# A recurrence and two layers on one core: a new order of the slots in the chunk periods

## The chip, the cores and the metric

One Trainium2 chip, one core of it. The metric is the device time of one execution in microseconds; the kernel is one program with one launch.

## What is computed

A recurrence over 768 positions for 4 x 8 heads of 40 channels, then two feed-forward layers on its output. Cut to what matters:

```python
for t in range(S):                     # S = 768, state is 40 x 40 per head
    y[:, :, t] = einsum('bhd,bhde->bhe', rt, state)
    Sa = einsum('bhde,bhe->bhd', state, at)
    state = state * wt[:, :, None, :] - einsum('bhd,bhe->bhde', Sa, bt) \
            + einsum('bhd,bhe->bhde', vt, kt)
x = y.transpose(0, 2, 1, 3).reshape(3072, 320)
h = x @ w_in;   x = square(relu(h)) @ w_out      # layer 0, 2048 hidden
h = x @ w_in2;  out = (h * cos(h)) @ w_out2      # layer 1
```

All inputs are drawn anew per seed; the weights of the layers come as 64-bit floats and are turned into 32-bit ones on the chip.

## The kernel before, in words

The 768 positions are cut into 12 chunks of 64. For each chunk the kernel forms decay products (`decay`, scans on DVE), products of the inputs with one another (`gt`, line 407, PE, tile pgt, then two masked multiplications into ga on DVE), stores parts of ga to DRAM (`gt_out`, Ls), loads them back in another layout (`solve_load`, L) and inverts 32 x 32 triangles (`solve`: 31 pairs of a product ttmp, line 448, and a sum T, line 451, each waiting for the one before, all on DVE). The result goes through DRAM again (`solve_store`, `load_t`) and is merged with two sets of small PE products (`merge`, tiles pw and pt). Then `state` takes four groups of heads through five steps each: pq, px, pu, py, pm on PE, with copies on ACT after pq, px and pm and multiplications on DVE after pu (into mov) and py (into MT, sz, yt). `pmat` (tile pp) makes a further operand. `y_store` writes the chunk's output.

All of it is written out by hand, no scheduler reorders it: `period(c)` is cut into 42 slots, and the calls `at(t, f, ...)` say what is issued in slot t. In period c the state of chunk c, the solve of chunk c+1 and the first steps of chunks c+2 and c+3 are issued. Each engine takes its instructions strictly in this order, so an instruction that waits holds up all that stands behind it on its engine. That goes for the DMA queue of SP too, on which all loads and stores of the periods stand.

Three further streams run beside it, slot by slot:

- The weights. `first`, `rest` and `second` (all through `stages`) load a piece, clamp it (ACT, then DVE), join the bits (DVE), add (POOL, tile u, line 179) and end it: for layer 0 by `split` (ACT into ws, line 206, and POOL), for layer 1 by a store to w2f. The tuples give the slot of each step within a job.
- The solve's links. `rate[t]` is the credit of a slot: after each operation that another part issues on DVE, one link of the solve follows, up to the credit.
- The layers (`Mlp.stream`). From slot FIRST of period 2 on, each slot issues RATE = 64.2/42 units of the stream. A unit of layer 0 is two PE products of 512 columns; a step has 8 units: 8 products into h, the activation (three operations on ACT, gh, and gl on POOL), and 8 products po of the step before the last. A block is 512 tokens (two chunks) and 16 steps; at its end the next block's input is split (xh on ACT, xl on DVE), once `load_x` has brought it and `ready` allows it.

After the last period the rest of the stream runs alone: layer 0 to its end, then layer 1 (lines 839 and 785).

Of the kernel before, what the change touches and what calls it, by code (L numbers as in the profile page):

```python
# [154 lines left out]
class Weights:  # L155
# [57 lines left out]
    def first(self, last=NF):  # L213
# [3 lines left out]
        def job(f):  # L217
# [17 lines left out]
            for t, c0, n in ((5, 0, 384), (6, 384, DM)):  # L235
                out.append((t, lambda c0=c0, n=n: begin(c0, n)))
                if self.raw:
                    out += [(t + 1, lambda c0=c0, n=n: self.bits(st["w"][:, c0:c0 + n], st[c0])),
                            (t + 2, lambda c0=c0, n=n: self.add(st["w"][:, c0:c0 + n], st[c0], st[c0]))]
                out.append((t + 2, lambda c0=c0: self.split(st["dst"], st[c0], c0)))  # L240
            return out
# [3 lines left out]
    def pieces(self, nm, tiles, period, end):  # L245
# [4 lines left out]
        def job(f, c0, n):  # L250
            st = {}

            def load():
                st["w"] = self.p.tile([128, 256, 2], I32, tag="w", name="w", bufs=2)[:, 0:n]
                self.load(nm, f, st["w"], c0)

            def clamp():
                st["u"] = self.p.tile([128, 256], F32, tag="u", name="u", bufs=2)[:, 0:n]
                self.clamp(st["w"], st["u"])

            return [(0, load), (5, clamp), (6, lambda: self.bits(st["w"], st["u"])),
                    (7, lambda: self.add(st["w"], st["u"], st["u"])), (period + 4, lambda: end(f, c0, st["u"]))]

# [18 lines left out]
class Attn:  # L282
# [159 lines left out]
    def solve(self):  # L442
        nc, L, T = self.nc, self.L, self.T
        for j in range(31):
            r, n = j // 2 + 1, 31 - j
            tmp = self.p2.tile([128, 136], F32, tag="ttmp", name="ttmp", bufs=1)
            tv = tmp[:, 0:r * n].rearrange("p (a b) -> p a b", b=n)
            nc.vector.tensor_tensor(tv, T[:, 0:r, j:j + 1].to_broadcast([128, r, n]),  # L448
                                    L[:, j:j + 1, j + 1:32].to_broadcast([128, r, n]), op=ALU.mult)
            yield  # L450
            nc.vector.tensor_tensor(T[:, 0:r, j + 1:32], T[:, 0:r, j + 1:32], tv, op=ALU.add)  # L451
            yield
        self.tn = L[0:64, 0:16].rearrange("p a b -> p (a b)").rearrange("p (i k) -> p i k", k=16)
        nc.vector.tensor_copy(self.tn, T[0:64].rearrange("p k i -> p i k"))
        yield
# [421 lines left out]
ALONE = 2  # L877
FIRST, RATE = 23, 64.2 / 42


class Program:
# [52 lines left out]
    def run(self):  # L934
# [46 lines left out]
        for k in range(10):  # L981
            self.vec.credit = 6
            if k in (3, 4, 5, 6, 7, 9):
                step(g1)
# [3 lines left out]
            if k in (1, 3, 5):  # L988
                step(self.w1)
            self.vec.finish()  # L990
        self.vec.credit = 100
        self.vec.finish()
        A.solve_store()
        A.load_t()
# [14 lines left out]
    def period(self, c):  # L1009
# [9 lines left out]
        for half in range(2):  # L1019
            for k in range(5):  # L1020
                for q in range(2):
                    at(20 * half + 4 * k + 2 * q, step, st[2 * half + q])
        for h, t0 in enumerate((5, 6) if c == 0 else (2, 4) if more else (4, 12)):
            mg = A.merge(h)
            at(t0, step, mg)
            at(t0 + 2, step, mg)
        at(2, A.rv_load, c, 2)
        at(6, A.rv_load, c, 3)
        at(6, A.mov_load, c, 2)
        at(9, A.pmat, c, 2)  # L1030
        at(13, A.mov_load, c, 3)
        at(15, A.pmat, c, 3)
        at(17, A.y_store, c, 0)
        at(37, A.y_store, c, 1)
        if more:
            early = c < ALONE
            for t in (0, 1, 1, 2, 3, 3) if early else (0, 1, 2, 3, 5, 6):
                at(t, step, self.gts[c + 1])
            at(2, A.gt_in, c + 1, 0, 0)
            at(3, A.gt_in, c + 1, 0, 1)  # L1040
            at(3 if early else 5, A.gt_out, c + 1, 1, 0)
            at(4 if early else 6, A.gt_out, c + 1, 1, 1)
            at(7, A.gt_in, c + 1, 1, 0)
            at(10, A.gt_in, c + 1, 1, 1)
            first = 9 if early else 13
            at(first - 3, A.solve_load, c + 1)
            for t in range(first, 36):
                rate[t] = 3 if t % 4 == 0 else 2 
                if not early:
                    rate[t] = 2 if t in (28, 30, 32, 34) else 3  # L1050
            rate[36] = 100
# [4 lines left out]
            at(26, A.mov_load, c + 1, 0)  # L1056
            at(29, A.pmat, c + 1, 0)
            at(33, A.mov_load, c + 1, 1)
            at(36, A.pmat, c + 1, 1)
        if c + 2 < nch:  # L1060
# [19 lines left out]
        for t in range(42):  # L1080
            if more and t == (9 if c < ALONE else 13):
                self.vec.chain = A.solve()
# [110 lines left out]
```

## Time and profile before

| | us |
|---|---|
| median of three runs | 1301.7 (1300.75 to 1304.37) |
| the profiled execution | 1310.03 |
| its span, first to last instruction | 1308.2 |
| PE busy (as modelled) | 1119.5, 86% |
| DVE busy | 858.8, 66% |
| ACT busy | 703.2, 54% |
| POOL busy | 489.7, 37% |
| mean granted TensorE clock, of full speed | 0.907 |

The twelve periods end at about 875 us, the layers alone take the rest. Shares over the whole span mix these two parts and should be read for each apart. PE's matmuls overlap and their ends are modelled, so a busy PE can still have room.

### The profile page before, as it was taken

Reading aid. Unit: us, or ns where it says so; the run is one execution under the profiler, and the core shown is the slowest. Engines: PE = TensorE matmul, PEld = TensorE weight load, DVE = VectorE, ACT = ScalarE, POOL = GpSimd, SP = SyncE. Lnnn points to the kernel's source line nnn. Section 1 sums busy time; section 2 is a strip of 40 time slices with the busy share of each in tenths; the row PEclk is TensorE's granted clock in tenths of the full one; section 3 lists DMA queues with packets and bytes.
Section 4 is the critical chain, followed back from the end, with each engine's and each line's share of the span. In section 5 each row is a group of like instructions: output and inputs, shape, how many; then the busy total and the mean of one; then the engine's idle time right before and its main releaser. Section 6 shows DMA issues by size and latency. Waiting matters only on the chain.

```text
span 1308.2 us, 27144 instructions
## 1 busy us (share of the span) xinstructions
PE 1119.5 (86%) x10242; PEld 898.7 (69%) x10242; DVE 858.8 (66%) x2014; ACT 703.2 (54%) x1492; POOL 489.7 (37%) x503
## 2 busy tenths in 40 slices
PE   3255638599888988898989899999999999999997
PEld 2244537466656766675757676678889999999996
DVE  7979787778869786979698859411088343434432
ACT  4224554366555656474647466546565565656554
POOL 4434370435232424233232422223487333333332
PEclk9985555689889989898989999999999999999999
DMA  6482835536374738374746463413040010101000
GB/s 175 89 173 84 188 90 130 113 72 137 80 163 102 158 82 171 98 146 96 162 116 136 104 145 86 96 35 133 9 124 26 21 45 1 45 1 45 1 21 24
DMA packets 281169, 121.75 MB, mean 93 GB/s; under 512 B 231013, under 2 KB 259173, under 8 KB 279885
## 3 DMA queue, kind: packets, MB, share of 16 engines
q1 hardware_dynamic: 279195, 119.24, 38.8%
q8 instruction: 83, 1.36, 0.5%
q10 hardware_dynamic: 1834, 0.69, 0.2%
q14 instruction: 57, 0.47, 0.1%
HBM read 91.31 MB, written 28.57 MB: 92 GB/s over the span
## 4 chain that ended last, share of the span: by engine, by line
PE 53%; DVE 22%; DMA 8%; SPq 6%; issue 5%; ACT 3%; POOL 2%; DVEq 0%; ACTq 0%; POOLq 0%
PE h L839 23%; PE pt L785 13%; PE po L795 8%; DVE T L451 7%; DVE ttmp L448 6%; SPq L437 4%; DVE u L142 3%; DMA L<-Ls 2%; DVE mov L142 2%; PE pgt L407 2%; DMA Ls<-ga 2%; PE pu L581 2%; PE py L591 1%; PE px L573 1%; DMA mov<-vt 1%
## 5 line engine op out<-in xcount | busy, mean ns | idle before, releaser
L839 PE MATMUL h<-xh,ws 128*128 128x512 f32 x960 | 342.5, 418 | 5.5 <-ACT g L693 4.3
L839 PE MATMUL h<-xl,ws 128*128 128x512 f32 x576 | 238.1, 413 | 4.5 <-DVE xl L142 4.5
L839 PEld LDWEIGHTS h<-xh,ws 128*128 128x128 f32 x960 | 185.6, 196 | 49.9 <-ACT g L693 6.6
L696 POOL TENSOR_TENSOR gl<-g,gh 128x512 fp32r<-128x512 f32 x96 | 126.1, 1314 | 226.9 <-ACT gh L695 192.5
L724 POOL TENSOR_TENSOR gl<-g,gh 128x512 fp32r<-128x512 f32 x96 | 124.9, 1301 | 191.4 <-ACT gh L723 163.8
L179 POOL TENSOR_TENSOR u<-u,w 128x256 int32<-128x256 int32 (+2 forms) x104 | 75.8, 729 | 280.0 <-issue 88.4
L448 DVE TENSOR_TENSOR ttmp<-T,L 128x126 f32<-128x126 f32 (+22 forms) x372 | 133.9, 360 | 31.1 <-DMA L<-Ls 23.4
L795 PE MATMUL po<-gh,ws 128*128 128x512 f32 x480 | 146.3, 417 | 0.0
L451 DVE TENSOR_TENSOR T<-T,ttmp 128x126 f32<-128x126 f32 (+22 forms) x372 | 135.5, 364 | 7.8
L142 DVE SCALAR_TENSOR_TENSOR g<-n,h 128x512 f32<-128x512 int32 x96 | 66.0, 687 | 103.2 <-ACT n L704 100.4
L693 ACT ACTIVATE g<-h 128x512 f32<-128x512 f32 x96 | 57.1, 595 | 138.9 <-PE h L839 137.7
L839 PEld LDWEIGHTS h<-xl,ws 128*128 128x128 f32 x576 | 112.7, 196 | 27.2 <-DVE xl L142 7.0
L785 PE MATMUL pt<-ws,gh 128*128 128x320 f32 x768 | 128.1, 308 | 0.5 <-DVE g L142 0.4
L785 PEld LDWEIGHTS pt<-ws,gh 128*128 128x128 f32 x768 | 119.9, 188 | 8.3 <-DVE g L142 0.6
L142 DVE TENSOR_SCALAR u<-u 128x256 f32<-128x256 f32 (+2 forms) x208 | 70.7, 340 | 79.3 <-ACT u L167 78.5
L704 ACT ACTIVATE n<-h 128x512 int32<-128x512 f32 x96 | 57.3, 596 | 119.9 <-PE h L839 119.9
L407 PE MATMUL pgt<-at,cin 40*128 40x104 f32 x768 | 73.9, 336 | 46.0 <-POOL at L387 34.0
L142 DVE TENSOR_TENSOR g<-g,h 128x512 f32<-128x512 f32 x96 | 65.8, 685 | 71.2 <-ACT g L708 71.1
L795 PEld LDWEIGHTS po<-gh,ws 128*128 128x128 f32 x480 | 88.4, 193 | 22.8 <-DVE o L142 0.3
L407 PEld LDWEIGHTS pgt<-at,cin 40*128 40x128 f32 x768 | 63.6, 236 | 57.2 <-POOL at L387 34.9
L795 PE MATMUL po<-gl,ws 128*128 128x512 f32 x288 | 91.3, 409 | 0.0
L581 PE MATMUL pu<-xsb,tt 64*64 64x104 f32 x384 | 55.8, 300 | 36.6 <-DVE mov L142 30.5
(96 smaller groups left out, 2313.4 us busy)
## 6 DMA issues: line engine op xcount, KB each, us to landing
rv<-rv SPq DMA_DIRECT2D x48, 256.0 KB
cin<-cin SPq DMA_DIRECT2D x11, 832.0 KB
w<-moe SPq DMA_DIRECT2D x12, 704.0 KB
w<-moe SPq DMA_DIRECT2D x40, 160.0 KB
Ls<-ga SPq DMA_DIRECT2D x48, 128.0 KB
L<-Ls SPq DMA_DIRECT2D x48, 128.0 KB
wr<-w2f SPq DMA_DIRECT2D x16, 352.0 KB
w<-moe SPq DMA_DIRECT2D x20, 256.0 KB
```

Source lines behind the costliest of these rows:

```text
L142: fn(*args, **kwargs)
L179: self.nc.gpsimd.tensor_tensor(t.bitcast(I32), u.bitcast(I32), w[:, :, 0], op=ALU.add)
L407: nc.tensor.matmul(pv[par][:, j], self.kb[r0:r0 + 40, p0 + j].rearrange("p h b -> p (h b)"), self.at[r0:r0 + 40, p0 + j], start=True, stop ...
L448: nc.vector.tensor_tensor(tv, T[:, 0:r, j:j + 1].to_broadcast([128, r, n]), L[:, j:j + 1, j + 1:32].to_broadcast([128, r, n]), op=ALU.mult)
L451: nc.vector.tensor_tensor(T[:, 0:r, j + 1:32], T[:, 0:r, j + 1:32], tv, op=ALU.add)
L581: nc.tensor.matmul(uv[64:128, j], tt[0:64, 4 * g + j], xs[0:64, j], start=True, stop=True)
L696: self.later.append((2, lambda: nc.gpsimd.tensor_tensor(gl, g, gh, op=ALU.subtract)))
L704: nc.scalar.activation(n, h, AF.Copy, bias=0.25, scale=float(np.float32(1.0 / (2.0 * np.pi))))
L724: nc.gpsimd.tensor_tensor(gl, g, gh, op=ALU.subtract)
L785: nc.tensor.matmul(self.pos[j][:, 0:DM], x[:, 128 * j:128 * j + 128], wo[:, DM * ws:DM * ws + DM], start=(f == 0 and x is gh and ws == 0), ...
L795: nc.tensor.matmul(self.pos[m], wo[:, 128 * ws:128 * ws + 128], x, start=(f == 0 and k in (0, 2, 4)), stop=(f == NF - 1 and k in (5, 6, 7)))
L839: nc.tensor.matmul(h, wi[:, ws], x[:, kt], start=(k == 0), stop=(k == 7))
```

## The change

It changes only the slots in which things are issued, and one name (`solve` writes `eng` for `nc.vector`, the same engine). The parts:

1. Weights: `split` of the first pieces two slots later; in the other pieces clamp, bits and add one slot earlier, the end (split or store) one slot later.
2. `gt` in four quarters of three steps: three quarters (nine steps) at the end of the period before instead of two, one at the head. The first period's third quarter moves into the prologue.
3. The two groups of a half, and the two halves of `merge`, are issued in the same slot.
4. `solve_load` in slot 6 and the solve from slot 9 in all periods (before: slots 10 and 13 from period 2 on), with 2 or 3 links a slot to slot 35.
5. The layers start in slot 9 of period 2 instead of 23; `load_x` and `ready` one slot later.

The core of the diff:

```diff
-                out.append((t + 2, lambda c0=c0: self.split(st["dst"], st[c0], c0)))
+                out.append((t + 4, lambda c0=c0: self.split(st["dst"], st[c0], c0)))
...
-            return [(0, load), (5, clamp), (6, lambda: self.bits(st["w"], st["u"])),
-                    (7, lambda: self.add(st["w"], st["u"], st["u"])), (period + 4, lambda: end(f, c0, st["u"]))]
+            return [(0, load), (4, clamp), (5, lambda: self.bits(st["w"], st["u"])),
+                    (6, lambda: self.add(st["w"], st["u"], st["u"])), (period + 5, lambda: end(f, c0, st["u"]))]
...
-FIRST, RATE = 23, 64.2 / 42
+FIRST, RATE = 9, 64.2 / 42
...
-                    at(20 * half + 4 * k + 2 * q, step, st[2 * half + q])
-        for h, t0 in enumerate((5, 6) if c == 0 else (2, 4) if more else (4, 12)):
+                    at(20 * half + 4 * k, step, st[2 * half + q])
+        for h, t0 in enumerate((5, 5) if c == 0 else (2, 2) if more else (4, 12)):
...
-            at(t0 + 2, step, mg)
+            at(t0 + (4 if c and more else 2), step, mg)
...
-            for t in (0, 1, 1, 2, 3, 3) if early else (0, 1, 2, 3, 5, 6):
+            for t in (0, 1, 2):
                 at(t, step, self.gts[c + 1])
...
-            at(3 if early else 5, A.gt_out, c + 1, 1, 0)
-            at(4 if early else 6, A.gt_out, c + 1, 1, 1)
+            at(3, A.gt_out, c + 1, 1, 0)
+            at(3, A.gt_out, c + 1, 1, 1)
...
-            first = 9 if early else 13
-            at(first - 3, A.solve_load, c + 1)
-            for t in range(first, 36):
-                rate[t] = 3 if t % 4 == 0 else 2 
-                if not early:
-                    rate[t] = 2 if t in (28, 30, 32, 34) else 3
+            at(6, A.solve_load, c + 1)
+            for t in range(9, 36):
+                rate[t] = 3 if t % 3 == 0 else 2
...
-            at(36, A.compact_a, c + 2, 1)
+            at(28, A.compact_a, c + 2, 1)
...
-            for t in (28, 30, 32, 33, 36, 37):
+            for t in (24, 25, 26, 32, 33, 34, 36, 37, 38):
                 at(t, step, self.gts[c + 2])
...
-            if c % 2 == 0 and c and t == 1:
+            if c % 2 == 0 and c and t == 2:
                 self.M.load_x(0, c // 2 - 1)
-            if c % 2 == 0 and t == (FIRST - 5 if c == 2 else 4):
+            if c % 2 == 0 and t == (FIRST - 3 if c == 2 else 5):
```

On SP's queue, in the head of period 4, before (xf is the input of a block, Ls<-ga the stores of `gt_out`, cin the load of the chunk after next, L the loads of `solve_load`, w and w2f the weights):

```order
L653 DMA xf_3584<-xs_59 64x4x128 x2
L510 DMA rv_3623<-rv 128x512
L278 DMA w2f_121<-u_3571 128x160
L421 DMA Ls_3293<-ga_3557 64x8x64
L183 DMA w_3712<-moe2 128x512
L510 DMA rv_3753<-rv 128x512
L518 DMA mov_3755<-vt 64x4x40 x2
L421 DMA Ls_3293<-ga_3557 64x8x64
L338 DMA cin_91<-cin 104x2048
L278 DMA w2f_121<-u_3714 128x160
L434 DMA T_3827<-kti 128x512
L437 DMA L_3826<-Ls_3293 32x32x32 x4
```

and now:

```order
L653 DMA xf_3715<-xs_59 64x4x128 x2
L421 DMA Ls_3301<-ga_3534 64x8x64 x2
L510 DMA rv_3806<-rv 128x512
L518 DMA mov_3808<-vt 64x4x40 x2
L434 DMA T_3812<-kti 128x512
L437 DMA L_3811<-Ls_3301 32x32x32 x4
L439 DMA l21_119<-Ls_3301 32x16x32 x2
L183 DMA w_3822<-moe2 128x512
L278 DMA w2f_121<-u_3652 128x160
L338 DMA cin_91<-cin 104x2048
```

The loads of L stood behind the load of cin and now stand ahead of it; the two stores of ga stand together, right behind the loads of xf.

On DVE, where the solve of period 5 begins, before (MT, sz and yt follow py; mov<-pu follows pu):

```order
L142 TENSOR_TENSOR mov<-pu,kc 64x416 x2
L142 TENSOR_TENSOR MT_111<-py,MT_111 104x160
L142 TENSOR_TENSOR sz<-py,sz 104x256
L142 TENSOR_TENSOR MT_111<-MT_111,lam_93 104x160
L142 TENSOR_TENSOR yt<-sz,lam_95 104x256
L142 TENSOR_SCALAR u<-u 128x128
L448 TENSOR_TENSOR ttmp<-T,L 128x31
L451 TENSOR_TENSOR T<-T,ttmp 128x31
```

and now:

```order
L142 SCALAR_TENSOR_TENSOR cin<-cin,kc 104x260
L142 TENSOR_TENSOR mov<-pu,kc 64x416 x4
L142 TENSOR_TENSOR mov<-pp,kc 64x4x64 x2
L142 TENSOR_SCALAR u<-u 128x256
L142 RECIPROCAL lam_94<-cin 104x4
L448 TENSOR_TENSOR ttmp<-T,L 128x31
L142 TENSOR_TENSOR lam_94<-lam_94 104x4x63
L451 TENSOR_TENSOR T<-T,ttmp 128x31
```

The first link stood behind the first group's py operations; now it stands ahead of them, behind all four pu multiplications.

## Rows read from the trace of the kernel before

**Rows 1.** The page, part 4: the chain that ended last, by engine.

```profile
PE 53%; DVE 22%; DMA 8%; SPq 6%; issue 5%; ACT 3%; POOL 2%; DVEq 0%; ACTq 0%; POOLq 0%
```

**Rows 2.** The chain in order of time, in the tail: start, us, what.

```profile
904.70 1.81 PE po L795 x8
906.51 1.81 PE h L839 x8
```

**Rows 3.** Windows: us; busy (instructions) of PE, PEld, DVE, ACT, POOL; PEclk; DMA; GB/s.

```profile
208.00:276.00 68.00, 49.72 (x595) 38.49 (x591) 49.47 (x144) 31.23 (x79) 19.38 (x24) 0.65 0.54 119
...
348.00:420.00 72.00, 62.60 (x710) 45.57 (x705) 56.19 (x150) 43.45 (x102) 22.14 (x22) 0.91 0.59 135
420.00:486.00 66.00, 60.32 (x694) 44.26 (x694) 55.26 (x146) 37.06 (x87) 21.48 (x21) 0.95 0.54 118
...
875.00:958.00 83.00, 83.00 (x367) 68.25 (x366) 12.43 (x20) 48.78 (x80) 35.69 (x31) 1.00 0.24 77
```

**Rows 4.** Windows of period 5, the same columns.

```profile
427.00:441.00 14.00, 14.00 (x242) 10.42 (x242) 8.35 (x20) 11.32 (x28) 3.77 (x4) 1.00 0.67 158
441.00:451.00 10.00, 10.00 (x118) 7.14 (x113) 8.42 (x15) 4.26 (x10) 5.36 (x5) 1.00 0.88 165
451.00:486.00 35.00, 29.32 (x276) 21.27 (x276) 31.60 (x99) 15.33 (x37) 10.27 (x11) 0.90 0.35 89
486.00:494.00 8.00, 8.00 (x92) 6.22 (x83) 6.38 (x13) 7.57 (x19) 4.25 (x5) 1.00 0.83 137
```

**Rows 5.** Timeline of DVE, period 5: start, us, instruction [idle before, what ended it].

```profile
427.48 1.06 DVE L142 TENSOR_TENSOR ga<-pgt,kc 128x416 f32<-128x416 f32 x2
...
439.72 1.21 DVE L142 TENSOR_TENSOR mov<-pu,kc 64x416 f32<-64x416 f32 x2 [3.52 <-PE pu L582]
...
441.46 0.86 DVE L142 TENSOR_TENSOR mov<-pp,kc 64x256 f32<-64x256 f32 x2 [0.33 <-PE pp L530]
...
450.95 0.56 DVE L448 TENSOR_TENSOR ttmp<-T,L 128x31 f32<-128x31 f32 x1 [0.54 <-DMA L<-Ls]
```

**Rows 6.** Waits, whole run: who for whom, us in total, times, longest us.

```profile
ACT ws L206 <- POOL u L179: 112.7, 32, 14.1
...
POOL cin L380 <- DMA cin<-cin: 50.4, 7, 13.5
...
DVE ttmp L448 <- DMA L<-Ls: 23.4, 9, 5.0
...
DVE MT L142 <- PE py L593: 8.4, 12, 1.2
```

**Rows 7.** Timeline of ACT, period 4: the split of a block and an activation.

```profile
382.12 1.65 ACT L667 ACTIVATE xh<-xf 128x512 fp32r<-128x512 f32 x3
383.67 0.58 ACT L693 ACTIVATE g<-h 128x512 f32<-128x512 f32 x1
384.28 0.63 ACT L694 ACTIVATE g<-g 128x512 f32<-128x512 f32 x1
```

**Rows 8.** Timeline of SP's queue, head of period 5.

```profile
436.44 0.61 SPq L421 DMA_DIRECT2D Ls<-ga  x1
437.49 0.35 SPq L338 DMA_DIRECT2D cin<-cin  x1
...
440.79 6.39 SPq L437 DMA_DIRECT2D L<-Ls  x4
```

**Rows 9.** Timeline of PE, head of period 5.

```profile
430.17 1.14 PE L407 MATMUL pgt<-at,cin 40*128 40x104 f32 x16
```

**Rows 10.** Timeline of DVE in the solve of period 5.

```profile
462.56 1.24 DVE L448 TENSOR_TENSOR ttmp<-T,L 128x120 f32<-128x120 f32 x1
...
464.15 0.30 DVE L448 TENSOR_TENSOR ttmp<-T,L 128x133 f32<-128x133 f32 x1
```

**Rows 11.** Timeline of POOL at the same time.

```profile
462.33 1.32 POOL L696 TENSOR_TENSOR gl<-g,gh 128x512 fp32r<-128x512 f32 x1
```

**Rows 12.** Waits between 66 and 132 us, period 0.

```profile
POOL cin L380 <- DMA cin<-cin: 13.5, 1, 13.5
```

More of the change, by code (lines that the diff above doesn't have):

```diff
@@ L442, in solve @@
     def solve(self):
-        nc, L, T = self.nc, self.L, self.T
+        eng, L, T = self.nc.vector, self.L, self.T
         for j in range(31):
@@ L447, in solve @@
             tv = tmp[:, 0:r * n].rearrange("p (a b) -> p a b", b=n)
-            nc.vector.tensor_tensor(tv, T[:, 0:r, j:j + 1].to_broadcast([128, r, n]),
+            eng.tensor_tensor(tv, T[:, 0:r, j:j + 1].to_broadcast([128, r, n]),
                                     L[:, j:j + 1, j + 1:32].to_broadcast([128, r, n]), op=ALU.mult)
             yield
-            nc.vector.tensor_tensor(T[:, 0:r, j + 1:32], T[:, 0:r, j + 1:32], tv, op=ALU.add)
+            eng.tensor_tensor(T[:, 0:r, j + 1:32], T[:, 0:r, j + 1:32], tv, op=ALU.add)
             yield
         self.tn = L[0:64, 0:16].rearrange("p a b -> p (a b)").rearrange("p (i k) -> p i k", k=16)
-        nc.vector.tensor_copy(self.tn, T[0:64].rearrange("p k i -> p i k"))
+        eng.tensor_copy(self.tn, T[0:64].rearrange("p k i -> p i k"))
         yield
@@ L982, in run @@
             self.vec.credit = 6
-            if k in (3, 4, 5, 6, 7, 9):
+            if k in (3, 4, 5, 6, 7, 8):
                 step(g1)
@@ L989, in run @@
                 step(self.w1)
+            if k > 7:
+                step(g1)
             self.vec.finish()
@@ L992, in run @@
         self.vec.finish()
+        step(g1)
         A.solve_store()
@@ L1029, in period @@
         at(6, A.mov_load, c, 2)
-        at(9, A.pmat, c, 2)
-        at(13, A.mov_load, c, 3)
-        at(15, A.pmat, c, 3)
+        at(8, A.pmat, c, 2)
+        at(14, A.mov_load, c, 3)
+        at(16, A.pmat, c, 3)
         at(17, A.y_store, c, 0)
@@ L1035, in period @@
         if more:
-            early = c < ALONE
-            for t in (0, 1, 1, 2, 3, 3) if early else (0, 1, 2, 3, 5, 6):
+            for t in (0, 1, 2):
                 at(t, step, self.gts[c + 1])
             at(2, A.gt_in, c + 1, 0, 0)
-            at(3, A.gt_in, c + 1, 0, 1)
-            at(3 if early else 5, A.gt_out, c + 1, 1, 0)
-            at(4 if early else 6, A.gt_out, c + 1, 1, 1)
-            at(7, A.gt_in, c + 1, 1, 0)
+            at(4, A.gt_in, c + 1, 0, 1)
+            at(3, A.gt_out, c + 1, 1, 0)
+            at(3, A.gt_out, c + 1, 1, 1)
+            at(8, A.gt_in, c + 1, 1, 0)
             at(10, A.gt_in, c + 1, 1, 1)
-            first = 9 if early else 13
-            at(first - 3, A.solve_load, c + 1)
-            for t in range(first, 36):
-                rate[t] = 3 if t % 4 == 0 else 2
-                if not early:
-                    rate[t] = 2 if t in (28, 30, 32, 34) else 3
+            at(6, A.solve_load, c + 1)
+            for t in range(9, 36):
+                rate[t] = 3 if t % 3 == 0 else 2
             rate[36] = 100
@@ L1056, in period @@
             at(26, A.mov_load, c + 1, 0)
-            at(29, A.pmat, c + 1, 0)
-            at(33, A.mov_load, c + 1, 1)
-            at(36, A.pmat, c + 1, 1)
+            at(28, A.pmat, c + 1, 0)
+            at(34, A.mov_load, c + 1, 1)
+            at(38, A.pmat, c + 1, 1)
         if c + 2 < nch:
@@ L1080, in period @@
         for t in range(42):
-            if more and t == (9 if c < ALONE else 13):
+            if more and t == 9:
                 self.vec.chain = A.solve()
```

## The prediction

> **What bounds the kernel now.** I read the page first, then the windows from one solve to the next, then one period on each engine. The chain of waits splits the span: PE 53%, DVE 22%, the rest issue and DMA [rows 1]. The first part is the twelve chunk periods, the second the layers alone. In the second part PE has nothing to wait for: eight products of 1.81 us after eight of 1.81 us [rows 2], so a step of layer 0 (16 products, 8 units of the stream) takes 3.62 us and **a unit 0.453 us**.
>
> In the periods no engine is full. From one solve's end to the next there are 72 and 66 us, of which DVE is busy 56.2 and 55.3 [rows 3]. Where does it idle? I cut period 5 in four [rows 4]: its head 427 to 441 (DVE 8.35 of 14), 441 to 451 (8.42 of 10), the solve 451 to 486 (31.60 of 35) and the end 486 to 494 (6.38 of 8). In the solve DVE is the bound: 99 operations with hardly a gap. In the head it is not: PE is shown busy for all 14.00 us and ACT for 11.32, and DVE waits 3.52 us for pu [rows 4, 5]. So a period is the head, set by PE and ACT, plus the solve, set by DVE; between them stands a wait of its own, the solve's first product for the matrix L: 23.4 us in nine waits, at most 5.0 [rows 6].
>
> **The change part by part.**
>
> *Layers from slot 9.* Stream work begins 14 slots earlier in period 2 at 64.2/42 units a slot: 21.4 units more are done when the periods end. No block is short of its input for them: with 33 slots of period 2 and nine whole periods the stream stands at about 628 units, and the five blocks that can be ready hold 645. The tail loses 21.4 x 0.453 = **9.7 us**. The same units now run in period 2, whose granted clock is 0.65, a mix of the two levels 1.2 and 2.4 GHz, against 0.91 to 0.95 later [rows 3]; at the lower level a unit costs twice. DVE is busy there only 49.5 of 68 us and PE 49.7, so most is covered. Bounds: 0, and +9.7 (no cover at all); with them come 2.7 chains of three ACT operations of about 0.6 us and one split xh of 1.65 [rows 7]. I take **+3**.
>
> *The solve at slot 9, its loads at slot 6.* In period 5 the store of ga is issued at 436.44, the load of cin at 437.49, the loads of L begin at 440.79 and hold SP for 6.39 us; DVE's first product then starts at 450.95 after a wait of 0.54 [rows 5, 8]. In the change both stores stand in slot 3, the L loads in slot 6 and so ahead of the cin load, and the first product in slot 9. The distance in slots from store to product is about as before (6 to 7), but DVE has four pu products and two pp products, 3.3 us by their rows, all in slot 8 ahead of it, and the 104 x 2048 load of cin no longer stands ahead of L in the DMA queues. L should be there within about 10 us of its first load (440.79 to 450.95 is the row) and DVE should need as long. Bounds: all 23.4 us saved, or none. I take two thirds, since these nine waits differ much (5.0 at most, 2.6 on average): **-15**. The 62 operations of the solve themselves cost the same at rate 2.33 as at 3.
>
> *A quarter of the products at the period's end.* Per period 16 recorded products pgt, 1.14 us on PE [rows 9], and two DVE multiplications, 1.06 us [rows 5], leave the head for slots 36 to 38. Both ends are stretches in which PE is shown busy throughout (14.00 of 14, 8.00 of 8) [rows 4], so I price it at **0**; bounds -1.1 and +1.1 in each of nine periods. Should the end have no cover, the next pq waits.
>
> *Groups in pairs.* Each group keeps four slots from step to step, so the time to hide a round trip stays; DVE finds two products in a row. What would be late is py for MT, now eight operations together at slots 12 and 32: this wait is 8.4 us in twelve now [rows 6]. In slot 12 DVE has seven links of the solve ahead of it that were not there. **0**, bounds -5 and +8.
>
> *The block's split moves into the head.* A block and two periods are 129 and 128.4 units, so the place where a block ends stays put: near slot 15 of even periods before, slots 3 to 5 now. There ACT, which with PE sets the head, gets xh, 1.65 us [rows 7], while DVE, the bound where it stood, is rid of xl. The load of x, four issues on SP in slot 2, is now ahead of the stores of ga in slot 3 and delays them. Bounds per even period: -2 (xl fills idle) and +4; I take +1, in four periods **+4**.
>
> *Splits and stores later.* ACT waits for POOL's sum in front of ws, 112.7 us in 32 waits, by the code all in the prologue and the first four periods [rows 6]. With splits two slots after the sum (one slot later for the rest) ACT passes on. DVE idles 18.5 of the 68 us from 208 to 276 [rows 3], only some of it for ACT: bounds 0 and -20, I take **-5**. The clamps stand a slot earlier, with one slot less for the DMA; nothing.
>
> *The solve beside POOL.* A product of the solve (128x120) took 1.24 us while POOL ran gl for 1.32 us; the next one, larger, took 0.30 [rows 10, 11]. So a POOL operation beside the solve costs DVE up to 0.94 us. Links in slots 9 to 13 meet the two cin multiplications of slots 10 and 12, which stood beside waits of DVE so far: 0 to 2 x 0.94 x 9 = +17, and since cin comes late from its load and ran beside slots 12 to 16 before too, I take **+2**.
>
> The Trainium skill, "SBUF — State Buffer", section Who interferes with whom, has this as a lock: a DVE instruction with two SBUF inputs and a GpSimd one that reads SBUF share a port, and the second to issue blocks until the first is done. The rows agree in kind, 1.24 us beside 1.32. By that rule taken whole, for every POOL operation that the longer solve meets, it speaks against this change; what it would then come to is the third rival.
>
> **Sum:** -9.7 + 3 - 15 + 0 + 0 + 4 - 5 + 2 = -20.7 us. The profiled execution took 1310.0 us (span 1308.2, 1.8 around it), 0.6% above the median of the three runs, 1301.7; the differences are taken off the median: **1281 us**, its own range 1272 to 1290.
>
> **Rivals.**
>
> 1. *The wait for L comes along.* Store, load and solve all moved by about the same slots, so DVE arrives early again. For it: same distances, and the head may get shorter. Against: cin is behind L now. Then the 15 falls away, with 5 us gained from ACT's waits and 9.7 from the tail: about 1295; if other waits shrink a little, 1290. I name **1293**.
>
> 2. *SP held ahead of cin: slower.* The L loads held SP 6.39 us [rows 8]. Standing in slot 6 they now hold back the cin load of slot 7 and the weight loads. POOL waits for cin before its first multiplication already, 50.4 us in seven, and the longest, 13.5, is in period 0, where the loads had this order before [rows 6, 12]: 6.3 more than the mean of 7.2. Behind it on POOL stand the sums u and the gl of the layers, and for gl waits PE. It decides when POOL comes later than the next gl is due, one step of the stream (8 units, some 5 slots) on. If half of 6.3 us is passed on in each of nine periods, +28; with the tail's -9.7 and the other terms unhurt but the 15, **1320**. Against: a gl has two steps of time.
>
> 3. *POOL takes it all.* Both cin multiplications and the gl between them meet links in all nine periods: 3 x 0.94 x 9 = 25 us in place of my 2. 1281 + 23 = **1304**, no change. For it: the rows of the collision. Against: DVE stood in the same collisions in period 5 (31.60 busy includes them).
>
> 4. *The head gets shorter too.* Fewer products in the head, and DVE's 5.65 idle us there [rows 4] shrink by 2 in eight periods: 1281 - 16 = **1265**.
>
> That the layers would not in fact get ahead (a block not ready) I rule out by the count of units above; a stall of three slots is made up at three units a slot.
>
> **How the numbers follow.** Forecast 0.52, rival 1 0.20, rival 2 0.12, rival 3 0.08, rival 4 0.08. What a measurement can tell from no change is 0.3%, 3.9 us: 1297.8 to 1305.6. Faster: forecast, rival 4 and four fifths of rival 1, 0.76. Same: rival 3 and the rest of rival 1, 0.12. Slower: 0.12. The range 1262 to 1304 holds all but rival 2 and a part of rival 3's and rival 4's outer ends.
>
> **What would show it.** The stretch after the last period should be 9.7 us shorter (it runs from 875 to 1308 now; its first 83 us [rows 3]). The wait of ttmp for L should fall from 23.4 to under 10 us, ACT's for POOL in front of ws by more than half, and POOL's for cin should stay near 50; windows of odd periods should lose about 2 us, even ones less. The prediction is wrong if the wait for L stays over 20 us, if POOL's wait for cin doubles and gl stops PE, or if period 2 grows by more than 8 us.

## The result and the profile after

The changed kernel took 1284.9 us (median of 4 executions, 1280.97 to 1287.12) against 1302.7 us (4 executions): ratio 0.9869, 95% interval 0.9842 to 0.9897. A second set (run a_again below) gave 0.9830 (0.9799 to 0.9862). That is 17 to 22 us less; the forecast was 20.7 less. The profiled execution took 1284.09 us, its span is 1282.3.

The page's first part and the clock line:

```profile
span 1282.3 us, 27055 instructions
PE 1082.7 (84%) x10242; PEld 902.6 (70%) x10242; DVE 862.1 (67%) x2014; ACT 700.7 (55%) x1492; POOL 489.6 (38%) x503
PEclk9995655889899999999889989999999999999998
```

The waits of the whole run of the changed kernel (who for whom, us in total, times, longest), beside [rows 6]:

```profile
POOL cin L380 <- DMA cin<-cin: 70.1, 10, 12.8
...
ACT ws L206 <- POOL u L179: 46.4, 20, 7.8
...
DVE mov L142 <- PE pp L530: 22.7, 10, 3.6
...
DVE ttmp L448 <- DMA L<-Ls: 5.9, 2, 4.9
```

ttmp's wait for L fell from 23.4 to 5.9 us and ACT's for POOL from 112.7 to 46.4, as forecast. Two of those that rose: POOL's for cin, from 50.4 to 70.1, and mov's for pp, which stood at 7.4 us in eight before, to 22.7.

Windows of periods 2, 4 and 5 and of the first 75 us of the layers alone (columns as in [rows 3], whose windows they answer to):

```profile
207.00:276.00 69.00, 55.23 (x660) 45.45 (x660) 58.83 (x147) 38.62 (x96) 23.77 (x28) 0.77 0.53 117
...
344.00:413.00 69.00, 58.22 (x702) 45.70 (x702) 56.78 (x150) 42.18 (x99) 22.88 (x22) 0.95 0.60 140
413.00:479.00 66.00, 60.22 (x707) 47.28 (x706) 54.67 (x146) 38.30 (x91) 23.44 (x23) 0.91 0.55 120
857.00:932.00 75.00, 74.75 (x331) 61.36 (x330) 13.16 (x22) 44.26 (x73) 33.66 (x30) 1.00 0.26 83
```

Layer 0 still runs alone for 75 us after the last period, where it ran for 83. Period 2 grew by 1 us while DVE's busy time in it rose from 49.47 to 58.83. The even period 4 lost 3 us, the odd period 5 nothing. I had expected the opposite of the last two.

Period 5, cut as in [rows 4] (head, start of the solve, solve, end):

```profile
423.00:437.00 14.00, 14.00 (x242) 11.21 (x242) 8.16 (x20) 11.87 (x28) 4.00 (x4) 1.00 0.79 170
437.00:447.00 10.00, 7.05 (x93) 5.60 (x94) 9.82 (x25) 3.62 (x10) 5.74 (x5) 0.93 0.72 152
447.00:480.00 33.00, 30.17 (x297) 23.63 (x296) 31.64 (x91) 19.29 (x48) 12.81 (x12) 0.91 0.30 79
480.00:488.00 8.00, 8.00 (x81) 6.14 (x79) 5.87 (x11) 3.22 (x7) 2.27 (x2) 0.80 0.91 154
```

DVE's timeline in it (start, us, instruction, [idle before, what ended it]):

```profile
434.32 2.45 DVE L142 TENSOR_TENSOR mov<-pu,kc 64x416 f32<-64x416 f32 x4 [2.08 <-PE pu L582]
...
437.88 0.16 DVE L448 TENSOR_TENSOR ttmp<-T,L 128x31 f32<-128x31 f32 x1
```

and SP's queue:

```profile
423.93 1.27 SPq L421 DMA_DIRECT2D Ls<-ga  x2
...
428.85 3.90 SPq L437 DMA_DIRECT2D L<-Ls  x4
...
434.03 0.46 SPq L338 DMA_DIRECT2D cin<-cin  x1
```

The loads of L now begin 9.0 us ahead of the first product, which does not wait. But compare the ends. Before, the solve of period 5 ran from 450.95 to 486.5, some 35.6 us; now it runs from 437.88 to 479.0, some 41.1 us. It starts 5.2 us sooner after the end of the last solve (25.4 against 30.6 us) and takes 5.5 us longer.

That cut, done in every period, is the measure used below. A period runs from the end of one solve (the copy of line 454) to the end of the next; **lead** is its part up to the next solve's first product (ttmp of 128x31), **solve** the rest. Means over even periods 4, 6, 8 and odd periods 3, 5, 7, 9, worked out from the timelines of each profiled execution, in us:

| kernel | even: lead + solve | odd: lead + solve | period 2 | last solve to layer 1 |
|---|---|---|---|---|
| before | 32.5 + 38.6 = 71.1 | 31.8 + 35.9 = 67.7 | 68.4 | 136.9 |
| changed | 25.5 + 43.4 = 68.9 | 24.0 + 42.1 = 66.0 | 69.1 | 124.4 |
| e1, changed, layers from 23 | 24.8 + 48.6 = 73.4 | 24.0 + 41.8 = 65.8 | 67.2 | 131.8 |
| f1, before, layers from 9 | 37.1 + 37.2 = 74.3 | 31.8 + 36.8 = 68.5 | 72.7 | 129.1 |
| f2, changed, block's split at 15 | 24.6 + 53.8 = 78.4 | 23.7 + 42.5 = 66.2 | 69.4 | 125.6 |
| e4, changed, solve from 13 | 32.3 + 37.7 = 70.0 | 30.3 + 35.7 = 66.0 | 68.1 | 125.9 |
| h2, before, layers from 9, quarter moved | 33.0 + 38.3 = 71.3 | 29.2 + 37.7 = 66.9 | 67.6 | 128.3 |
| h1, changed, quarter back in the head | 26.3 + 43.1 = 69.4 | 24.2 + 42.6 = 66.8 | 69.4 | 123.9 |
| e5, changed, without pairs | 24.7 + 44.7 = 69.4 | 23.6 + 43.2 = 66.8 | 70.2 | 129.1 |

The sums are of unrounded times. These are single executions, within 1% of their medians; the span of before that was profiled was itself 0.6% above its median, so differences of a microsecond a period to "before" carry nothing.

### The profile page after: what moved, and what is told of

The parts are those of the page before. It is cut to its first block, busy times and chain, and to the rows that moved or that the text cites. A ratio compares the mean times of both kernels' runs of the same rounds, so it can differ in the third digit from the quotient of the medians.

```text
span 1282.3 us, 27055 instructions
## 1 busy us (share of the span) xinstructions
PE 1082.7 (84%) x10242; PEld 902.6 (70%) x10242; DVE 862.1 (67%) x2014; ACT 700.7 (55%) x1492; POOL 489.6 (38%) x503
## 5 line engine op out<-in xcount | busy, mean ns | idle before, releaser
L839 PE MATMUL h<-xh,ws 128*128 128x512 f32 x960 | 336.2, 413 | 14.6 <-ACT g L693 14.4
L448 DVE TENSOR_TENSOR ttmp<-T,L 128x126 f32<-128x126 f32 (+22 forms) x372 | 144.0, 387 | 13.2 <-DMA L<-Ls 5.9
L795 PE MATMUL po<-gh,ws 128*128 128x512 f32 x480 | 137.5, 408 | 4.6 <-ACT g L693 2.4
L407 PE MATMUL pgt<-at,cin 40*128 40x104 f32 x768 | 78.9, 340 | 68.8 <-POOL at L387 40.6
L142 DVE TENSOR_SCALAR u<-u 128x256 f32<-128x256 f32 (+2 forms) x208 | 73.3, 353 | 79.1 <-ACT u L167 78.1
L407 PEld LDWEIGHTS pgt<-at,cin 40*128 40x128 f32 x768 | 67.4, 239 | 77.8 <-POOL at L387 42.5
L142 DVE TENSOR_TENSOR g<-g,h 128x512 f32<-128x512 f32 x96 | 65.8, 686 | 71.1 <-ACT g L708 71.1
L795 PE MATMUL po<-gl,ws 128*128 128x512 f32 x288 | 86.8, 405 | 0.0
L380 POOL TENSOR_TENSOR cin<-cin 104x512 f32<-104x512 f32 x46 | 55.1, 1209 | 82.1 <-DMA cin<-cin 70.1
```

The costliest lines, as they stand in the source:

```text
L142: fn(*args, **kwargs)
L407: nc.tensor.matmul(pv[par][:, j], self.kb[r0:r0 + 40, p0 + j].rearrange("p h b -> p (h b)"), self.at[r0:r0 + 40, p0 + j], start=True, stop ...
L448: eng.tensor_tensor(tv, T[:, 0:r, j:j + 1].to_broadcast([128, r, n]), L[:, j:j + 1, j + 1:32].to_broadcast([128, r, n]), op=ALU.mult)
L795: nc.tensor.matmul(self.pos[m], wo[:, 128 * ws:128 * ws + 128], x, start=(f == 0 and k in (0, 2, 4)), stop=(f == NF - 1 and k in (5, 6, 7)))
L839: nc.tensor.matmul(h, wi[:, ws], x[:, kt], start=(k == 0), stop=(k == 7))
```

## The experiments

Ratios are against the kernel before, run on the same chip, with 95% intervals. The changed kernel itself came to 0.9869 and 0.9830 in its two sets, so a difference of 0.004 between runs of two sets (5 us) can be the sets'.

The change moves more slots than the list of its parts names: those of `pmat` (9, 15, 29, 36 to 8, 16, 28, 38), and some of `mov_load` and `gt_in` by one. Of these only the last `pmat` is undone in a run (e8); the slots of the weights' other pieces are undone in none.

**The changed kernel again**, as the mark for the runs beside it.

> The changed kernel itself, timed again beside the kernels below: 0.987 of the kernel before, between 0.984 and 0.990 (1285 us).

0.9830 (0.9799 to 0.9862), 1282.7 us. Its profile has the same picture: L wait 3.2 us, cin 66.9, pp 21.0.

**e1: everything but the early start of the layers.**

```diff
-FIRST, RATE = 9, 64.2 / 42
+FIRST, RATE = 23, 64.2 / 42
```

> The changed kernel with the layers from slot 23 of period 2, as before (21.4 units fewer in the periods; the block's split moves back to mid period). By my terms: tail +9.7, period 2 -3, even periods' heads -4, so +2.7 us, about 1288. Rival: the early start is free and the place of the split doesn't matter, +9.7, about 1295. Second rival: period 2 pays for the early units in full, 0, about 1285.

**1.0003 (0.9981 to 1.0026)**, 1302.9 us: without the early start all the rest of the change together is worth nothing, and none of the three expectations (1285, 1288, 1295) came. Yet its wait for L is down to 9.6 us:

```profile
DVE ttmp L448 <- DMA L<-Ls: 9.6, 5, 3.7
```

The difference to the changed kernel is 20 us, twice the 9.7 of the tail. From last solve to layer 1 there are 7.4 us more (131.8 against 124.4), period 2 is 1.9 shorter; the rest lies in the even periods, 73.4 against 68.9, and there wholly in the solve (48.6 against 43.4). The odd ones are alike. An even period is one in which a block ends and its successor is split: in e1 near slot 15, amid the solve, in the changed kernel in the head. The window of period 8's solve and DVE's waits in it, e1:

```profile
641.90:690.70 48.80, 35.91 (x375) 28.03 (x375) 41.59 (x113) 24.23 (x58) 17.04 (x17) 0.85 0.44 106
```

```profile
PE h L839 <- DVE xl L142: 3.9, 1, 3.9
...
DVE u L142 <- ACT u L167: 5.6, 3, 3.3
```

and the changed kernel:

```profile
640.30:682.40 42.10, 37.12 (x372) 29.22 (x368) 38.88 (x110) 23.16 (x56) 17.18 (x17) 0.86 0.44 111
```

```profile
DVE u L142 <- ACT u L167: 0.5, 1, 0.5
```

Of the 6.7 us between them 2.7 are DVE's busy time (three xl and what they collide with) and 4.0 are idle. PE's h waits for xl; on ACT the clamp u stands behind work that waits for h; DVE's next step on u waits for the clamp, and the links of the solve stand behind that. In the whole run of the changed kernel PE never waits for xl. There the three xl of period 4 stand some 17 us after the end of the last solve, ahead of the next one:

```profile
360.58 1.90 DVE L142 TENSOR_TENSOR xl<-xf,xh 128x512 fp32r<-128x512 f32 x3 [0.51 <-ACT xh L667]
```

**f1: the early start alone, in the old order.**

```diff
-FIRST, RATE = 23, 64.2 / 42
+FIRST, RATE = 9, 64.2 / 42
```

(against the kernel before)

> The kernel before with one number of the change, FIRST = 9. New theory (all of the gain is the stream's start: 21.4 units out of the tail, and the block's end moved from slot 15 to the head of the even periods): -9.7 and about -3 in each of four even periods, 0.983 of before or 1283, as fast as the whole change. Rival, my terms as forecast: -9.7 + 3 + 4 = -3, 1300. Second rival: only the tail, -9.7, 1293.

**1.0071 (1.0044 to 1.0098)**, 1314.4 us: slower, where all three expectations were faster. The part on which the whole gain hangs costs 10 us when it stands alone. The way from last solve to layer 1 is 7.8 us shorter, as in the new order. But period 2 is 4.3 longer and the even periods 3.2, and the lead alone has grown (37.1 against 32.5) while the solve lost 1.4. DVE's timeline shows what stands in this lead. Before, in period 6, the last quarter's masked product ends 15.2 us after the end of the last solve:

```profile
501.13 0.57 DVE L142 TENSOR_TENSOR ga<-pgt,kc 128x416 f32<-128x416 f32 x1
```

In f1, in the same period, the split (xl, which waits for xh) stands ahead of it, and it ends 22.3 us after:

```profile
512.55 1.90 DVE L142 TENSOR_TENSOR xl<-xf,xh 128x512 fp32r<-128x512 f32 x3 [4.64 <-ACT xh L667]
...
515.47 0.57 DVE L142 TENSOR_TENSOR ga<-pgt,kc 128x416 f32<-128x416 f32 x1
...
532.25 1.04 DVE L448 TENSOR_TENSOR ttmp<-T,L 128x31 f32<-128x31 f32 x1 [4.94 <-DMA L<-Ls]
```

The stores of ga stand behind that product, the loads of L behind the stores, and the solve behind the loads. In the mean of periods 4, 6 and 8 the last ga ends 21.6 us after the last solve, 16.8 before: 4.8 later, and the lead is 4.6 longer. In the order of slots it is slot 4 (the next block made ready) against slots 5 and 6 (the last quarter's products into ga). So in the old head the block's split holds up the way to the solve; the solve, freed of the split, gives back less than the lead pays. A run of the old order with the split alone moved behind the last quarter was not made.

**f2: the new order, but the split held to slot 15.**

```diff
-            if c % 2 == 0 and t == (FIRST - 3 if c == 2 else 5):
+            if c % 2 == 0 and t == (FIRST - 3 if c == 2 else 15):
```

> The changed kernel with the next block made ready in slot 15 in place of 5 from period 4 on: the stream stands still until then and makes up for it at three units a slot, so that the units done by a period's end stay the same and only the place of the split of x moves. New theory: the place is worth 3 to 4.5 us in each of periods 4, 6, 8, 10, so +12 to +18, about 1297, and PE waits for xl again. Rival: the place is worth nothing, 1283, and the 20 us come from the units alone.

1.0089 (1.0057 to 1.0120), 1315.6 us, more than the 1297 expected; PE waits for xl again, 5.2 us in five. Only the solves of the even periods grow, to 53.8. They grow twice as much as in e1, since the stream also stands still for some ten slots here and catches up at three units a slot. So the run shows the place and the direction, and its size is not the split's alone.

**f3: the units of period 2's slots 9 to 22 issued late.** They are counted from slot 9 but run from slot 23 on, at up to three a slot.

```diff
-                self.acc -= self.mlp(min(int(self.acc), 3))
+                if c > 2 or t >= 23:
+                    self.acc -= self.mlp(min(int(self.acc), 3))
```

> The changed kernel with the stream's first units held back to slot 23 of period 2 and then made up for at three a slot: units and places of the splits from period 3 on as in the change, but no work of the layers in slots 9 to 22 of period 2. New theory: nothing lost, 1283 within 3 us, since period 2 only shifts its own work. Rival (PE's clock and the idle slots of period 2 are the gain): some 5 to 10 us lost, 1290.

0.9875 (0.9832 to 0.9918), 1286.5 us: no difference to the changed kernel that can be told, and e1's ratio lies above its interval. The interval reaches to 1293 us, so the rival's 5 us of loss are not excluded. But most of the gain does not lie in filling slots 9 to 22 of period 2, nor in PE's clock there (the granted clock of period 2 is 0.70 in f3 as in e1, 0.77 in the changed kernel). It lies in being 21 units ahead: a shorter tail and blocks that end elsewhere.

**e4: the solve from slot 13 and its loads in slot 10 again** (with the old rates, from period 2 on).

```diff
-            at(6, A.solve_load, c + 1)
-            for t in range(9, 36):
+            first = 9 if c < 2 else 13
+            at(first - 3, A.solve_load, c + 1)
+            for t in range(first, 36):
...
-            if more and t == 9:
+            if more and t == (9 if c < 2 else 13):
```

> The changed kernel with the solve's loads in slot 10 and its first link in slot 13 from period 2 on, three links a slot, as before. My theory, that the gain is the wait for L: the wait of ttmp for L rises from 5.9 back to some 20 us and the time by about 15, to 1300. Rival: with the stores now in slot 3 the loads in slot 10 find them landed, the wait stays under 8 us, and the time changes by less than 5 (1280 to 1290): then the earlier stores were what took the wait away, not the earlier solve.

0.9839 (0.9809 to 0.9869), 1284.7 us: the same as the changed kernel, as the rival had it. Its waits for L and cin:

```profile
POOL cin L380 <- DMA cin<-cin: 18.2, 5, 5.9
...
DVE ttmp L448 <- DMA L<-Ls: 1.8, 2, 1.0
```

The wait for L is gone with the solve in its old slot, so it was not the solve's slot that removed it. And the lead is 6 to 7 us longer, the solve 6 us shorter (32.3 + 37.7 against 25.5 + 43.4): the links end in slot 35 either way. An earlier first product spreads them over more slots, it does not end the solve sooner.

**h1 and h2: the quarter of the products.** h1 puts it back in the head of the changed kernel (with the prologue's extra steps removed); h2 moves it in the old order, together with the early start (with the prologue's extra steps and `compact_a` in slot 28).

```diff
-            for t in (0, 1, 2):
+            for t in (0, 1, 1, 2, 3, 3):
...
-            at(3, A.gt_out, c + 1, 1, 1)
+            at(4, A.gt_out, c + 1, 1, 1)
...
-            for t in (24, 25, 26, 32, 33, 34, 36, 37, 38):
+            for t in (24, 25, 26, 32, 33, 34):
```

(h1, against the changed kernel)

```diff
-FIRST, RATE = 23, 64.2 / 42
+FIRST, RATE = 9, 64.2 / 42
...
-            for t in (0, 1, 1, 2, 3, 3) if early else (0, 1, 2, 3, 5, 6):
+            for t in (0, 1, 2):
...
-            at(3 if early else 5, A.gt_out, c + 1, 1, 0)
-            at(4 if early else 6, A.gt_out, c + 1, 1, 1)
+            at(3, A.gt_out, c + 1, 1, 0)
+            at(3, A.gt_out, c + 1, 1, 1)
...
-            for t in (28, 30, 32, 33, 36, 37):
+            for t in (24, 25, 26, 32, 33, 34, 36, 37, 38):
```

(h2, against the kernel before)

> The changed kernel with the third quarter alone back in the head (slots 0 to 3, as periods 0 and 1 had it before); the first two quarters keep their new slots 24 and 32, so that no pgt stands beside the pair of pu in slot 28, where the kernel with half of the products moved back waited 47.6 us for PSUM tiles that DVE had not yet read. If those waits were all of its 31 us, this one is at 1283; if the head's room is what counts, the even periods go to 72 or more and the time to 1290 to 1300. My first pricing said 0.

> The kernel before with two parts of the change: FIRST = 9, and gt in quarters with the third at the period's end and the stores of ga in slot 3 (without pairs, without the weights' new slots, with the solve at 13). If room in the head is what lets the early start pay, these two alone give most of the gain: 1288 to 1292, near the changed kernel without pairs (1290), where FIRST = 9 alone gave 1314. Rival: the quarter does not matter without pairs, 1310.

h1: 0.9905 (0.9879 to 0.9930), 1290.0 us: by the two ratios of the changed kernel, 0.9869 and 0.9830, it is 5 to 10 us dearer (the interval of the first overlaps this one, that of the second doesn't). The time came as expected, but the even periods did not grow to 72: they take 69.4. DVE now waits for pgt, mostly in the head:

```profile
DVE ga L142 <- PE pgt L407: 13.5, 8, 4.5
```

against 1.1 us in one in the changed kernel. h2: 0.9958 (0.9940 to 0.9976), 1296.7 us, against f1's 1.0071: moving the quarter, with the stores that follow it, takes 15 us off in the old order with the early start. Expected was 1288 to 1292 and most of the whole gain; h2 has 5 to 6 us of the 17 to 22. The even periods come back from 74.3 to 71.3, where they were before (71.1), and not below. On DVE the last ga of period 6 now stands ahead of the split and ends 10.8 us after the last solve:

```profile
488.96 0.58 DVE L142 TENSOR_TENSOR ga<-pgt,kc 128x416 f32<-128x416 f32 x1
...
495.17 1.90 DVE L142 TENSOR_TENSOR xl<-xf,xh 128x512 fp32r<-128x512 f32 x3 [3.28 <-ACT xh L667]
```

In h1 the products in the head, in slots 0 to 3, stand ahead of the split (slot 5) too, so h1 does not undo this. The wait for L, h2 and then f1:

```profile
DVE ttmp L448 <- DMA L<-Ls: 4.8, 2, 2.5
```

```profile
DVE ttmp L448 <- DMA L<-Ls: 26.2, 8, 5.1
```

Solve and loads stand in their old slots here, and the cin load still goes ahead of L. So the stores of ga, two or three slots sooner because a quarter of the products no longer stands before them, are what removes the wait. The even lead falls from f1's 37.1 to 33.0, about where it was without the early start (32.5).

**e5: groups two slots apart again, halves of the merge too.**

```diff
-                    at(20 * half + 4 * k, step, st[2 * half + q])
-        for h, t0 in enumerate((5, 5) if c == 0 else (2, 2) if more else (4, 12)):
+                    at(20 * half + 4 * k + 2 * q, step, st[2 * half + q])
+        for h, t0 in enumerate((5, 6) if c == 0 else (2, 4) if more else (4, 12)):
...
-            at(t0 + (4 if c and more else 2), step, mg)
+            at(t0 + 2, step, mg)
```

> The changed kernel with the groups of the state two slots apart again and the halves of merge apart as before. What has to be told apart: with the old order the early start made the kernel slower (even periods 74.3 and 75.9 us with the block's end in the head), with the new one it gave 20 us (68.7 and 69.3). If pairs are what lets the head take the block's end, even periods go to 73 to 75 and the time to 1300 or more. Rival: pairs do nothing, 1283, and the quarter moved out of the head is what does it.

0.9901 (0.9872 to 0.9930), 1289.6 us: reckoned in the same way the pairs are worth 4 to 9 us, the lower end within what two sets can differ by. It lies between the two expectations, and even periods do not go to 73: they take 69.4, against 68.9. The solves are longer, 44.7 us in even and 43.2 in odd periods (changed: 43.4 and 42.1), the leads 0.4 to 0.8 shorter. Most of it lies behind the last solve, in the last period, which has no solve. The window from there to the last operation of the state on DVE (yt), e5 and then the changed kernel:

```profile
811.64:864.90 53.26, 50.28 (x538) 37.09 (x537) 13.69 (x35) 27.61 (x62) 11.70 (x12) 0.94 0.24 52
```

```profile
807.63:854.40 46.77, 45.29 (x535) 35.64 (x532) 13.71 (x36) 24.51 (x55) 11.25 (x11) 0.96 0.26 56
```

It takes 52.3 to 53.3 us in the four profiles without pairs (before, f1, h2, e5) and 44.9 to 48.4 in the ten with them. With the rest of layer 0, which is 1.7 us longer in the changed kernel, the way from last solve to layer 1 is 4.7 us longer in e5.

**e6: half of the products back in the head, on the old slots 28 to 37** (with the prologue's extra steps removed and the second store in slot 4, as in h1).

```diff
-            for t in (0, 1, 2):
+            for t in (0, 1, 1, 2, 3, 3):
...
-            for t in (24, 25, 26, 32, 33, 34, 36, 37, 38):
+            for t in (28, 30, 32, 33, 36, 37):
```

> The changed kernel with half of the products gt in the head again, in slots 0 to 3 as periods 0 and 1 had it before. If the quarter that left the head (1.14 us of PE and 1.06 of DVE there) is what made room, even periods go to 73 and the time to about 1300; and the stores of ga come later, so the wait for L returns in part (over 10 us). Rival, as I had priced it: 0, 1283.

1.0095 (1.0072 to 1.0117), 1313.8 us, far more than h1's quarter; the wait for L stayed small (4.4 us). A wait that the changed kernel does not have, and that is 0.3 us before, goes with it (47.6 us of it from period 3 on):

```profile
PE pgt L407 <- DVE mov L142: 75.1, 10, 11.7
```

In slot 28 a pgt now stands beside the pairs of pu and pp. These tiles share a pool of four in PSUM by the code, and PE holds still until DVE has read one. The run is no measure of the quarter; h1 was made in its place.

**e2: the splits of the first weights back to t + 2; e8: e2 and pmat of the coming chunk in slot 36 instead of 38.**

```diff
-                out.append((t + 4, lambda c0=c0: self.split(st["dst"], st[c0], c0)))
+                out.append((t + 2, lambda c0=c0: self.split(st["dst"], st[c0], c0)))
```

```diff
-            at(38, A.pmat, c + 1, 1)
+            at(36, A.pmat, c + 1, 1)
```

> The changed kernel with the first weights' split two slots after the clamped sum's start, as before. The prologue of the changed kernel ends its solve 5.1 us later than before (71.2 for 66.1), with a clamp on ACT waiting 15.3 us for POOL's ws. If the later split is the cause, the prologue gets its 5 us back; periods 0 and 1, which got 5 us shorter, lose what the later split gave them. Theory: prologue -5, periods 0 and 1 +4, in sum about -1 (1284). Rival, my term as forecast (later splits gain 5): +5, 1290. Second rival: only the prologue matters, -5, 1280.

> The changed kernel with two of its steps undone: the first weights' split two slots after the sum, and the last pmat in slot 36 in place of 38. In the changed kernel DVE waits 22.7 us in ten for PE's pp, most of it in slot 38, 7.4 in eight before. Theory: the wait in slot 38 goes and the periods, bound by DVE and PE there, get 1 to 2 us shorter in nine periods, so 1270 with the 1 us of the split. Rival: PE is as late for ga or pq instead, 1281 as with the split alone.

e2: 0.9807 (0.9776 to 0.9838), 1281.6 us, e8: 0.9858 (0.9830 to 0.9886), 1285.9 us. Neither can be told from the changed kernel: e2 ran beside a_again on one chip, and their intervals overlap over most of their width. In e2 ACT again waits for POOL:

```profile
ACT ws L206 <- POOL u L179: 95.7, 27, 16.1
```

twice the 46.4 us, for no time that can be told. The prologue gets its 5 us back: it ends at 71.2 us in the changed kernel and at 66.1 in e2 and before. Periods 0 and 1 lose little by it: 136.8 us in e2, 136.2 in the changed kernel, 141.9 before, so their gain is not that of these later splits. Where the rest of the 5 us goes no row shows: e2 is 4.5 us ahead at the start of period 2 and 0.6 at the end of the last solve. In the changed kernel's first 72 us the waits are:

```profile
ACT u L167 <- POOL ws L210: 15.3, 1, 15.3
DVE u L142 <- ACT u L167: 11.8, 1, 11.8
```

In e8, where 1270 was hoped for, the wait of mov for pp shrinks to 3.6 us in one, and DVE waits for pgt in its place:

```profile
DVE ga L142 <- PE pgt L407: 12.3, 9, 5.5
```

The wait moved from one tile to the other, as the rival had it. The wait for pp needs both the quarter at the period's end and pmat in slot 38: with the quarter back in the head it is 5.2 us (h1), with the quarter moved and pmat in slot 36 it is 3.1 (h2).

## Why the prediction was right, and which steps were not

The size and the direction held (-17 to -22 us against -20.7), and none of the rivals came. The terms did not hold one by one. Two large errors cancel, the solve's 15 us that were not there and the split's, which was +4 and came to -16; that the sum met is luck.

*Layers from slot 9: -9.7 and +3.* Right in kind, both sizes a little smaller: 7.4 us off the tail (e1 against changed), +1.9 in period 2.

*The block's split, +4.* Wrong in sign, and the largest miss. "ACT, which with PE sets the head, gets xh" priced the old head. In the old order the sign was right and the size too low: f1's even lead grew by 4.6 us for each +1 that I had set. And there it was not ACT's time for xh but what xl holds up behind it on DVE. In the new head the split costs 0.7 (25.5 against 24.8), and the solve is rid of 5.2: some 4.5 in each of the three even periods 4, 6, 8 and 2.3 in period 10 (60.6 us against e1's 62.9), 16 us in all. I had counted xl's busy time as what leaves the solve, not the chain behind it, xl to h to the clamp to u.

*The solve and the wait for L, -15.* The wait fell as forecast (23.4 to 5.9 us), but the step failed twice. Its cause was not the slot of the solve but the stores of ga (h2, e4). And a vanished wait was booked as time: in e1 it is down by 13.8 us and the kernel as slow as before. There the lead is 7.7 us shorter in even and odd periods alike, and the solve takes 10.0 and 5.9 longer. The chain runs through the order of the slots, and the last links stand in slot 35.

*A quarter of the products, 0.* Wrong: -5 to -10 in the new order (h1, the lower end within what two sets can differ by), -15 in the old one with the early start (h2 against f1, with the stores and `compact_a` earlier and the first two quarters on their new slots). "PE is shown busy throughout at both ends" was true, but the head is where ga's stores and the block's split stand, the end is not. What its place decides in the old order is whether the last quarter stands behind the split on DVE (the rows of f1 and h2). The wait forecast for a full end did come too, as mov's for pp, 7.4 to 22.7 us, with the new slot of pmat.

*Pairs, 0 (-5 to +8).* -4 to -9 by e5, at the bound or beyond it. I had looked at the periods with a solve; the last one, without, is where 4.7 us of it stand.

*Splits later, -5.* The wait that I watched fell by 66 us; in e2 49 of them are back and the time is the same.

*Solve beside POOL, +2.* The page's rows of ttmp and T in the changed kernel:

```profile
L448 DVE TENSOR_TENSOR ttmp<-T,L 128x126 f32<-128x126 f32 (+22 forms) x372 | 144.0, 387 | 13.2 <-DMA L<-Ls 5.9
L451 DVE TENSOR_TENSOR T<-T,ttmp 128x126 f32<-128x126 f32 (+22 forms) x372 | 136.5, 367 | 7.5
```

Together 280.5 us, where before has 133.9 + 135.5 = 269.4: +11, inside the bound of 17. It does not come from the slot: e4, with the solve from 13, has 284.6. The old order with the early start does not have it (f1, 267.5), and with the quarter moved too has little of it (h2, 273.4). Which part brings it was not separated.

*Rival 2* had its mechanism half: POOL's wait for cin rose by 20 us. With the loads in the old order (e4) it is 18.2, and the time the same, so what stood behind POOL cost nothing that can be told. (Its own sum, 1281 + 15 + 28, is 1324, not 1320.) *Rival 1* is excluded by the wait itself, *rivals 3 and 4* by the time, 1304 and 1265 against 1285.

So what is shown: the gain is one of combination. The early start alone costs 10 us, all the rest alone gives 0, both together -17 to -22. Against the kernel before, 12.5 us lie behind the last solve (136.9 to 124.4): 7 to 8 of the early start, about 5 of the pairs. In the new order the early start has two halves, a tail shorter by 7 us and blocks that end in the head of even periods (16 us). In the old order the second turns into a loss, and the rows put it on the order on DVE: the split stood ahead of the last quarter, and with it of the stores and of the solve. (That is read from the rows; the split was not moved by itself.) Moving the quarter takes 15 us off and brings the even periods back to where they were, no further.

What is not shown: which part makes the even periods shorter than before. Between h2 and the whole change lie 12 to 17 us; the pairs are worth 4 to 9 of them, mostly in the last period, the solve's slot nothing (e4), and the rest, the weights' and pmat's slots among it, was not separated. With the quarter back (h1) or the pairs undone (e5) the even periods stay at 69.4, so neither alone carries it. Which part makes the links dearer is open too.

## What to carry to other kernels

In an order written out by hand, price an edit on the head or the stretch that the other edits leave behind, not on the one in the trace, and name for each term which other part it leans on; one run with the part alone and one with all but that part tell more than the sum. Ask too what will stand behind a costly step on its own engine once it is moved: the split cost little by itself, and in the old order it held up the stores that the solve waits for. A wait is not time: ask what the engine does with it, and whether the end that counts is set by the operation or by its slot. Where a periodic side stream has a costly step, look at which place of the main period it falls on; a shift of the stream's start may move it out of the tightest stretch.

## What the runs showed of the hardware

DVE and POOL took turns for seven microseconds in e1, in the solve of period 4. DVE's timeline:

```profile
374.25 1.22 DVE L142 TENSOR_SCALAR u<-u 128x128 f32<-128x128 f32 x1 [1.19 <-ACT u L167]
375.40 1.25 DVE L448 TENSOR_TENSOR ttmp<-T,L 128x96 f32<-128x96 f32 x1
376.57 1.23 DVE L142 TENSOR_TENSOR xl<-xf,xh 128x512 fp32r<-128x512 f32 x1
377.72 2.38 DVE L451 TENSOR_TENSOR T<-T,ttmp 128x96 f32<-128x96 f32 x1
380.03 1.75 DVE L142 TENSOR_TENSOR xl<-xf,xh 128x512 fp32r<-128x512 f32 x1
381.70 0.27 DVE L448 TENSOR_TENSOR ttmp<-T,L 128x115 f32<-128x115 f32 x1
```

and POOL's:

```profile
374.11 1.29 POOL L696 TENSOR_TENSOR gl<-g,gh 128x512 fp32r<-128x512 f32 x1
375.36 1.18 POOL L380 TENSOR_TENSOR cin<-cin 104x512 f32<-104x512 f32 x1
376.50 0.75 POOL L179 TENSOR_TENSOR u<-u,w 128x256 int32<-128x256 int32 x1
377.21 2.77 POOL L380 TENSOR_TENSOR cin<-cin 104x512 f32<-104x512 f32 x2
379.94 1.28 POOL L696 TENSOR_TENSOR gl<-g,gh 128x512 fp32r<-128x512 f32 x1
```

A sum T of the solve took 2.38 us beside two POOL multiplications in a row, where a link of about its size takes 0.27 right behind them. That is more than the 0.94 us for which I had priced a collision: POOL's operations follow one another without a gap, and the DVE instruction outlasts both. The Trainium skill, "SBUF — State Buffer", section Who interferes with whom, gives the lock between the two engines as the cause; these rows agree with it. What I had not priced is the plain u<-u, which reads a single tensor: 1.22 us beside gl, where the same shape takes 0.21 in the changed kernel in a stretch in which POOL is idle:

```profile
344.76 0.21 DVE L142 TENSOR_SCALAR u<-u 128x128 f32<-128x128 f32 x1
```

The same section of the Trainium skill names this kind of instruction (tensor_scalar) among those that can take both ports and so contend with GpSimd, and the two rows agree.
